# A fused attention and two-layer-pair kernel: one-bank PSUM tiles, attention batches in pairs, and shifted priorities

## The chip, the cores and the metric

The kernel runs on one core of a Trainium2 chip. The metric is the device time of one execution in microseconds. The profile is taken from one execution of its own, whose time stands beside its span below.

The engines are called as in the profile: PE is TensorE (PEld its weight loads), DVE is VectorE, ACT is ScalarE, POOL is GpSimd, and SP is SyncE, which issues nearly all DMAs here.

## The reference

Attention over 4 batches, 8 heads, 768 positions, 64 numbers per head, in chunks of 32 queries. Each chunk sees 8 memory slots and its own window of 16 + 32 + 8 keys:

```
scores = (q_c @ k_full.T) / 8            # 32 queries x 64 keys
a      = exp(scores - max(scores))
a      = a / (sum(a) + 1e-9)
out_c  = a @ v_full
x      = out, as 3072 tokens x 512
h = x @ w_in;   g = s * relu(h)**2 + b;           x = g @ w_out     # 512 -> 2048 -> 512
h = x @ w_in2;  g = h * sigmoid(1.702 * h);       y = g @ w_out2    # 512 -> 2048 -> 512
```

The weights come as float64. All results are float32 and are wanted to nearly that precision, so large products are made as three products of rounded parts (high x high, high x low, low x high).

## The kernel before

**Order.** Nothing runs in the order in which the code lists it. The class `Plan` collects operations: each has a due value (`need`), the engines that could do it with an assumed duration, what it comes after, and the buffers it takes. `Plan.order` (L80) then plays the program through with these durations, and writes the instructions out in the order it finds. Among the operations that could start on an engine within `PATIENCE` of the earliest, it takes the one with the smallest latest time (`late`). Operations with two engines go to the one that would end them first (for instance copies out of PSUM, L248). An attention batch is marked `dense`, and no two dense batches may start within `SPACE` = 2.4 us of the plan's clock. Where the plan sees TensorE idle before the first real accumulation, it puts in filler matmuls on a zero tile (`idle`, L1304).

**Attention.** A tile is 128 queries of all 8 heads; there are 24. `attend` (L427) handles one of the first four tiles alone and the later ones two at a time. A tile goes through these steps: loads of k, q and v (L439); scores `sc` on TensorE (L454); masking of the edge; the maximum `top` and its subtraction on VectorE (L471, L474); the exponential in place in `qe` on ScalarE (L479); transposes `pp` (L487); a copy to `px` (L249); the sum `den` (L497, L500, L501); the values `o` (L515); the division (L520); transposes `xx` back (L529); then high and low part, `xh` (L249) and `xl` (L546). The scores or values of one tile are 32 matmuls in the order listings and 64 in the trace, each using a 64x32 part of the array. q and k each have one buffer for a pair of tiles, so the next pair's q can be loaded once the transposes and the sum have read the exponentials.

**First layers.** Tokens are taken in blocks of 512 (`b`), four tiles each. `step` (L628) does one 128-wide piece j of the hidden layer for a block: 12 matmuls into `ph` (L644), ScalarE and VectorE make the gate (L650, L657, L654 or L661), split it into `gh` (L665) and `gl` (L669), and 12 matmuls add into `accA`, `accB` (L677). The first two j are done in halves of 256 tokens, so that they can start with tiles 0 and 1. Blocks are visited in the order 0, 1 (j below 8), 1, 0 (j from 8), 2, 3. Each weight piece is brought to a rounded high part and a low part by ScalarE and VectorE (`words` and `prep`, L334 to L400: four steps on VectorE, of which L346 is the last), just before it is needed.

**Later layers.** The last third of the first pair of layers and all of the second go through a Winograd-like scheme over 2 x 2 blocks with seven products (`wino`, L961, four runs `s` = 0 to 3). Products go from one accumulator to the next by a ScalarE copy (`seed`, L1059). `outer_product` (L1152) makes the last products; `away` (L1187) adds two parts (L1194) and stores them (L1201).

**PSUM.** Of eight banks two are `h`, two are `accA` as one tile, two are `accB` as two one-bank tiles, two are `a` as one tile. Attention takes `a`, tiles 1 and 3 take `accA` (`SIDE`).

Of the kernel before, what the change touches and what calls it, by code (L numbers as in the profile page):

```python
# [32 lines left out]
WARM = 8  # L33
# [12 lines left out]
S_PE = 0.8  # L46
V_PE = 0.8

class Plan:
# [3 lines left out]
    AFTER = {"pe": 0.2, "act": 0.05, "dve": 0.05, "pool": 0.2, "sp": 0.1, "aq": 0.1, "none": 0.0}  # L53
    OVER = {"act": 0.09, "dve": 0.08}
    BEAT = 0.24
    SPACE = 2.4
# [23 lines left out]
    def order(self):  # L80
# [20 lines left out]
        for i in range(len(ops) - 1, -1, -1):  # L101
# [7 lines left out]
            late[i] = self.due.get(i, min(due))  # L109

# [7 lines left out]
        holds, packed = {}, [-9.0]  # L118
# [25 lines left out]
        while left:  # L144
# [29 lines left out]
            if i in self.dense:  # L174
                packed[0] = t
# [20 lines left out]
        for i, e in chosen:  # L196
            if e == "pe":
                idle = min(starts[i], first) - clock
                if idle > 0.3:
                    full.append((None, int((idle - 0.3) / self.BEAT)))  # L200
                clock = ends[i]
            full.append((i, e))
# [13 lines left out]
def attention_moe_moe(ctx: ExitStack, tc: tile.TileContext, q_t, k_w, v_w, w_in1, w_out1, s_b, w_in2, w_out2, out):  # L216
# [13 lines left out]
    ps_a = ctx.enter_context(tc.tile_pool(name="ps_a", bufs=1, space=PS))  # L230
# [62 lines left out]
    o_cold = op(-999, {"dve": 0.7}, chill, alloc=[("ys", "cold")])  # L293
    plan.due[o_cold] = -1000.0
    o_ident = op(-135, {"pool": 0.5}, lambda e: make_identity(nc, ident))
# [8 lines left out]
    op(-999, {"pe": 0.46 * WARM}, warm, after=[o_cold], alloc=[("h", "warm")], uses=["cold"])  # L304


    managers = {"gp": pool_g, "att": pool_a}
# [115 lines left out]
    def bank(name, u):  # L423
        T[name, u] = (ps_acc if u in SIDE else ps_a).tile([P, 2, 512], F32, tag="accA" if u in SIDE else "a", name=name)
        return T[name, u]

    def attend(u):  # L427
# [3 lines left out]
        one = len(plan.ops)  # L431

# [48 lines left out]
        def turn(i):  # L481
            def fn(e):
                if i == 0:
                    bank("pp", u)
                x = T["qe", g][:, u[i] % 2]
                for a in range(HP):
# [8 lines left out]
        def total(e):  # L495
            den = T["den", u] = att.tile([P, n * HP, 2], F32, tag="den", name="den", bufs=2)
            nc.vector.tensor_reduce(  # L497
                out=den.rearrange("p x h -> p (x h)"), in_=T["qe", g][:, sub].rearrange("p t a (h s) -> p (t a h) s", h=2),
                op=ALU.add, axis=AX.X)
# [863 lines left out]
```

## Time and profile before

| | |
|---|---|
| time, median of 3 runs | 1084.7 us (1083.78 to 1085.21) |
| the profiled execution | 1084.78 us |
| its span in the trace | 1083.0 us |
| PE busy | 1063.8 us (98%) |
| PEld busy | 908.4 us (84%) |
| DVE busy | 763.4 us (70%) |
| ACT busy | 598.5 us (55%) |
| DMA | 265.68 MB, mean 245 GB/s |

The span runs from the first instruction of the program to its last; what the device time has beyond it lies around it. Busy time of TensorE includes matmuls that overlap, since they are pipelined, so it hides short gaps: starts of neighbouring matmuls tell more.

### The profile page before, as it was taken

To read this page: it belongs to the slowest core of one execution; us is meant where nothing else is said; L and a number is where in the kernel's file an instruction comes from. 1 tells how busy PE (TensorE), PEld (TensorE's weight loads), DVE (VectorE), ACT (ScalarE), POOL (GpSimd) and SP (SyncE) were. 2 spreads that over 40 slices of the span, in tenths; PEclk is the share of its full clock that TensorE was granted. 3 is DMA by queue.
4 is the path that set the end of the run, shared out by engine and by line. 5 is a ranking of instruction groups with operands and counts; after the bars stand their busy time and mean duration, and the time that the engine had idled before them with its cause. 6 is when DMAs were issued, how large, how long until landed. Compare 5 with 4: busy or idle time off the path is not lost.

```text
span 1083.0 us, 21691 instructions
## 1 busy us (share of the span) xinstructions
PE 1063.8 (98%) x8588; PEld 908.4 (84%) x8588; DVE 763.4 (70%) x1155; ACT 598.5 (55%) x921; POOL 0.7 (0%) x6
## 2 busy tenths in 40 slices
PE   8899999999999999999999999999999999999998
PEld 6777887778877788788888777999888999888998
DVE  7898986778798658888999554995223985222944
ACT  5668755545666647688744665543355532454432
POOL 0000000000000000000000000000000000000000
PEclk9999999999999999999999999999999999999999
DMA  9988934658699964888978998867656766666662
GB/s 341 313 279 295 304 125 142 229 180 304 212 328 313 371 222 152 308 298 271 326 225 282 340 346 283 262 203 252 195 185 212 235 196 221 193 187 205 196 204 79
DMA packets 151541, 265.68 MB, mean 245 GB/s; under 512 B 14224, under 2 KB 65424, under 8 KB 151440
## 3 DMA queue, kind: packets, MB, share of 16 engines
q1 hardware_dynamic: 151152, 263.77, 72.9%
q8 instruction: 68, 1.11, 0.4%
q10 hardware_dynamic: 288, 0.52, 0.1%
q14 instruction: 33, 0.27, 0.1%
HBM read 190.84 MB, written 73.40 MB: 244 GB/s over the span
## 4 chain that ended last, share of the span: by engine, by line
PE 88%; DMA 2%; ACT 2%; DVE 0%; SPq 0%; issue 0%; DVEq 0%
PE ph L644 14%; PE pc L1166 10%; PE accA L677 7%; PE accB L677 7%; PE pd L1166 6%; PE pb L1166 6%; PE pc L1172 3%; PE pd L1015 3%; PE pd L1017 3%; PE pd L1016 3%; PE ph L1015 3%; PE ph L1017 3%; PE ph L1016 3%; PE pc L1015 2%; PE pc L1017 2%; PE pc L1016 2%
## 5 line engine op out<-in xcount | busy, mean ns | idle before, releaser
L1140 DVE TENSOR_TENSOR oj<-G,oj 128x1024 fp32r<-128x1024 f32 x72 | 87.9, 1222 | 51.3 <-ACT oj L1137 50.8
L1137 ACT CAST oj<-G 128x1024 fp32r<-128x1024 f32 x72 | 75.6, 1051 | 87.5 <-PE pd L1166 28.6
L650 ACT ACTIVATE r<-ph 128x512 f32<-128x512 f32 (+1 forms) x66 | 38.5, 583 | 75.3 <-PE ph L644 68.8
L1137 ACT CAST oq<-G 128x1024 fp32r<-128x1024 f32 x40 | 42.1, 1052 | 51.6 <-PE pc L1166 22.0
L1140 DVE TENSOR_TENSOR oq<-G,oq 128x1024 fp32r<-128x1024 f32 x40 | 48.9, 1222 | 27.3 <-ACT oq L1137 27.3
L1166 PE MATMUL pc<-wih,oj 128*128 128x256 f32 x336 | 62.4, 284 | 0.0
L665 ACT CAST gh<-r 128x512 fp32r<-128x512 f32 (+1 forms) x66 | 40.0, 606 | 37.4 <-PE accB L677 34.9
L1149 DVE TENSOR_TENSOR G<-G 128x1024 f32<-128x1024 f32 x48 | 57.2, 1220 | 0.4
L669 DVE TENSOR_TENSOR gl<-r,gh 128x512 fp32r<-128x512 f32 (+1 forms) x66 | 44.1, 668 | 17.3 <-ACT gh L665 16.7
L368 ACT ACTIVATE u<-st 128x512 f32<-128x512 f32 x64 | 42.6, 670 | 22.8 <-DMA st<-w_in 12.9
L1027 ACT ACTIVATE G<-ys 128x512 f32<-128x512 f32 x64 | 40.6, 634 | 24.9 <-DVE ys L1069 24.4
L1166 PE MATMUL pd<-wih,oj 128*128 128x256 f32 x288 | 53.8, 284 | 0.0
L1166 PEld LDWEIGHTS pc<-wih,oj 128*128 128x128 f32 x336 | 53.3, 192 | 0.0
L1166 PE MATMUL pc<-wil,oj 128*128 128x256 f32 x168 | 47.6, 284 | 0.0
L1166 PEld LDWEIGHTS pd<-wih,oj 128*128 128x128 f32 x288 | 45.9, 192 | 0.0
L1166 PE MATMUL pc<-wih,oq 128*128 128x256 f32 x240 | 45.7, 284 | 0.0
L380 DVE SCALAR_TENSOR_TENSOR u<-u,st 128x512 uint32<-128x512 uint32 x64 | 43.4, 685 | 2.4 <-ACT st L376 1.4
L1166 PE MATMUL pb<-wih,oj 128*128 128x256 f32 x240 | 44.7, 284 | 0.0
L386 DVE SCALAR_TENSOR_TENSOR u<-st,u 128x512 uint32<-128x512 uint32 x64 | 43.5, 686 | 0.5
L376 ACT ACTIVATE st<-st 128x512 uint32<-128x512 uint32 x64 | 42.9, 672 | 0.8 <-DMA st<-w_out 0.7
L657 ACT ACTIVATE r<-r 128x512 f32<-128x512 f32 (+1 forms) x66 | 40.8, 618 | 1.6
L677 PE MATMUL accA<-gh,woh 128*128 128x512 f32 (+1 forms) x132 | 41.5, 390 | 0.0
(253 smaller groups left out, 3011.0 us busy)
## 6 DMA issues: line engine op xcount, KB each, us to landing
wih<-wodh SPq DMA_DIRECT2D x112, 256.0 KB, 2.9
wil<-wodl SPq DMA_DIRECT2D x112, 256.0 KB, 3.4
wih<-wch SPq DMA_DIRECT2D x96, 256.0 KB, 3.5
wil<-wcl SPq DMA_DIRECT2D x96, 256.0 KB, 3.9
st<-w_in SPq DMA_DIRECT2D x32, 512.0 KB, 6.5
st<-w_out SPq DMA_DIRECT2D x32, 512.0 KB, 6.0
k<-k_w SPq DMA_DIRECT2D x24, 512.0 KB, 5.4
v<-v_w SPq DMA_DIRECT2D x24, 512.0 KB, 5.9
```

Source lines behind the costliest of these rows:

```text
L380: nc.vector.scalar_tensor_tensor(out=u, in0=u, scalar=3, in1=T["st", i][:, :, 0], op0=ALU.logical_shift_left, op1=ALU.bitwise_or)
L386: nc.vector.scalar_tensor_tensor(out=u, in0=T["st", i][:, :, 1], scalar=0x80000000, in1=u, op0=ALU.bitwise_and, op1=ALU.bitwise_or)
L644: nc.tensor.matmul(T["ph", i], T[win][x][:, k * P:(k + 1) * P], T["x", m, b][y][:, k, r], start=seen_["hid"] == 1, stop=seen_["hid"] == 3 ...
L669: nc.vector.tensor_tensor(out=gl, in0=T["r", i], in1=gh.bitcast(F32), op=ALU.subtract)
L677: nc.tensor.matmul(T["acc", group, k // 2][:, k % 2][:, r], T[wout][x][:, k * P:k * P + P], T["g", i][y], start=fresh and (x, y) == (0, 0) ...
L1015: nc.tensor.matmul(ph, wh, xh, start=first and i == 0, stop=False, skip_group_check=True)
L1016: nc.tensor.matmul(ph, wh, xl, start=False, stop=False, skip_group_check=True)
L1017: nc.tensor.matmul(ph, wl, xh, start=False, stop=i == 1, skip_group_check=True)
L1137: nc.scalar.copy(out=T[kh], in_=g_of(ty, z))
L1140: nc.vector.tensor_tensor(out=T[kl], in0=g_of(ty, z), in1=T[kh].bitcast(F32), op=ALU.subtract)
L1149: o_raw[out, x] = [op(need, {"dve": 1.22}, lambda e: nc.vector.tensor_tensor(out=g_of(out, z), in0=g_of(a, z), in1=g_of(b, z), op=o), afte ...
L1166: nc.tensor.matmul(a, lt[:, z], rh, start=first and t % 2 == 0 and x == 0, stop=p == HALF - 1 and x == 2, skip_group_check=True)
```

## The change

- `WARM` goes from 8 to 9; the cold tile is set by one memset, without the cast; a new operation `table` runs an exponential of one column on ScalarE as soon as that tile is there.
- `HEADED = 1`: for tile 0 the subtraction, the exponential and the sum are replaced. VectorE scales the maximum by -1/8 (`bias`), and ScalarE does eight exponentials of 64 columns straight from PSUM with that bias, each adding up its sum (`heads`). The transposes of that tile may go two at a time. The later steps are as before.
- The spacing `SPACE` of dense batches is gone. Instead the plan charges 0.09 for going into one and 0.25 for coming out of one, with batches of 0.66 instead of 0.8.
- `bank` and `pair`: attention has its own pools `ps_a` and `ps_x`; when attention is over they are closed, and their banks become one-bank tiles `accA0`, `accA1`, `a0`, `a1` as `accB` already was.
- The last `outer_product` of the program is cut into two halves, and the last stores into one half and two quarters (`last`).
- Assumed durations change, and the table `SHIFTS` adds a number to the latest time of stretches of operations, so that the plan chooses another order.

```diff
-WARM = 8
+WARM = 9
+HEADED = 1
-S_PE = 0.8
-V_PE = 0.8
+S_PE = 0.66
+V_PE = 0.66
+SHIFTS = (
+    (894, 1, 7.29), (671, 4, -0.76), (408, 16, -0.4), (1809, 256, 4.91), (804, 4, -3.27), (1733, 1, 26.29),
...
-    SPACE = 2.4
+    INTO, OUT_OF = 0.09, 0.25
...
+        for at, n, by in SHIFTS:
+            for i in range(at, min(at + n, len(ops))):
+                shift[i] += by
+        late = [x + y for x, y in zip(late, shift)]
...
-            if i in self.dense:
-                t = max(t, packed[0] + self.SPACE)
+            if e == "pe" and (i in self.dense) != packed[0]:
+                t += self.OUT_OF if packed[0] else self.INTO
...
     def chill(e):
-        cold = pp.tile([P, KT, 512], F32, tag="ys", name="cold")
-        T["cold"] = cold[:, 1].bitcast(F32R)
-        fill(e, cold[:, 0], 0.0)
-        nc.vector.tensor_copy(out=T["cold"], in_=cold[:, 0])
+        T["cold"] = pp.tile([P, KT, 512], F32, tag="ys", name="cold")[:, 0].bitcast(F32R)
+        fill(e, T["cold"].bitcast(F32), 0.0)
+
+    def table(e):
+        x = const.tile([P, 1], F32, name="one")
+        nc.scalar.activation(out=x, in_=T["cold"].bitcast(F32)[:, :1], func=AF.Exp)
...
     def bank(name, u):
-        T[name, u] = (ps_acc if u in SIDE else ps_a).tile([P, 2, 512], F32, tag="accA" if u in SIDE else "a", name=name)
+        T[name, u] = (ps_x if u in SIDE else ps_a).tile([P, 2, 512], F32, tag="s", name=name)
...
+        def bias(e):
+            nc.vector.tensor_scalar_mul(out=T["top", u], in0=T["top", u], scalar1=-SCALE)
+
+        def heads(a):
+            def fn(e):
+                if a == 0:
+                    T["den", u] = att.tile([P, n * HP, 2], F32, tag="den", name="den", bufs=2)
+                x, sc = T["qe", g][:, u[0] % 2], two("sc")
+                for h in range(2):
+                    nc.scalar.activation(out=x[:, a, h * SLOTS:h * SLOTS + SLOTS], in_=sc[:, h, a], func=AF.Exp, scale=SCALE,
+                                         bias=T["top", u][:, h, a], accum_out=T["den", u][:, a, h:h + 1])
+            return fn
...
     def pair(tag, name):
-        if tag == "accB":
-            return Banks([ps_acc.tile([P, 512], F32, tag=f"{tag}{n}", name=name) for n in range(2)])
-        return (ps_a if tag == "a" else ps_acc).tile([P, 2, 512], F32, tag=tag, name=name)
+        pool = {"accB": ps_acc, "accA": pools.get("ps_y"), "a": pools.get("ps_b")}[tag]
+        return Banks([pool.tile([P, 512], F32, tag=f"{tag}{n}", name=name) for n in range(2)])
...
+        def last(n, b, part, need, after, end):
+            held = ("turn", s) + BANKS[n]
+            lo, hi = (part, part + 1) if b else (0, 2)
+            z = slice(256 * lo, 256 * hi)
+
+            def fn(e):
+                nc.vector.tensor_tensor(out=spot(b)[:, z], in0=T[held][:, b][:, z], in1=spot(b)[:, z], op=ALU.add)
+
+            def store(e):
+                r = bp * 512 + b * 256
+                dst = out[r + lo * P:r + hi * P, 256:512].rearrange("(t p) d -> p t d", p=P)
+                nc.sync.dma_start(out=dst, in_=spot(b)[:, z].rearrange("p (t d) -> p t d", t=hi - lo))
...
-                    prev = [outer_product(n, p, here + 8 * p, key, d, prev + wait)]
+                    if s == len(SEVEN) - 1 and n == 2 and p == HALF - 1:
+                        prev = [outer_product(n, p, here + 8 * p + only, key, d, prev + wait, only) for only in range(2)]
+                    else:
+                        prev = [outer_product(n, p, here + 8 * p, key, d, prev + wait)]
```

What the change moves, at three places. The first is the start, on TensorE, before (`warm` and `idle` are matmuls on the zero tile; `sc`, `pp`, `o`, `xx` are the steps of attention; a row of 32 is one tile):

```order
L1304 MATMUL idle<-cold 128x512 x5
L301 MATMUL warm<-cold 128x512 x8
L454 MATMUL sc<-k,qe 32x64 x32
L1304 MATMUL idle<-cold 128x512 x7
L454 MATMUL sc<-k,qe 32x64 x32
L487 MATMUL pp<-ident,qe 128x128 x4
L1304 MATMUL idle<-cold 128x512 x3
L515 MATMUL o<-v,px 32x64 x32
L1304 MATMUL idle<-cold 128x512 x3
L487 MATMUL pp<-ident,qe 128x128 x4
L529 MATMUL xx<-ident,px 128x128 x4
```

The same engine and place in the changed kernel (a row of 64 is two tiles):

```order
L361 MATMUL warm<-cold 128x512 x9
L515 MATMUL sc<-k,qe 32x64 x32
L1427 MATMUL idle<-cold 128x512
L515 MATMUL sc<-k,qe 32x64 x32
L1427 MATMUL idle<-cold 128x512 x6
L561 MATMUL pp<-ident,qe 128x128 x8
L1427 MATMUL idle<-cold 128x512
L592 MATMUL o<-v,px 32x64 x64
L606 MATMUL xx<-ident,px 128x128 x8
```

Transposes, values and back-transposes of tiles 0 and 1 now each stand together; before, tile 0 was through its values ahead of tile 1's transposes.

The second place is tiles 8 and 9, on TensorE, during the first visit of block 1 with j from 8 on (`ph` and `wj` belong to the hidden layer), before:

```order
L454 MATMUL sc<-k,qe 32x64 x32
L644 MATMUL ph<-xh_348,wj 128x512 x4
L644 MATMUL ph<-xl_349,wj 128x512 x4
L454 MATMUL sc<-k,qe 32x64 x32
L644 MATMUL ph<-xh_348,wj 128x512 x4
```

And now:

```order
L515 MATMUL sc<-k,qe 32x64 x64
L735 MATMUL ph<-xh_387,wj 128x512 x8
L735 MATMUL ph<-xl_388,wj 128x512 x4
L735 MATMUL ph<-xh_387,wj 128x512 x4
L561 MATMUL pp<-ident,qe 128x128 x8
L735 MATMUL ph<-xl_388,wj 128x512 x4
L735 MATMUL ph<-xh_387,wj 128x512 x4
L592 MATMUL o<-v,px 32x64 x64
```

Eight large matmuls stood between the two scores; now the scores of both tiles stand together, and so do the values.

The third place is the end, on VectorE, before (`oj`, `oq` are split operands, `ys` holds the outputs, `pc` the last accumulator):

```order
L1140 TENSOR_TENSOR oj_11644<-G_5698,oj_11643 128x1024
L1182 TENSOR_TENSOR ys_10328<-pd_11533,ys_10328 128x512
L1182 TENSOR_TENSOR ys_10328<-pd_11534,ys_10328 128x512
L1194 TENSOR_TENSOR ys_10328<-ys_10328 128x512 x2
L1140 TENSOR_TENSOR oj_11673<-G_5698,oj_11672 128x1024
L1140 TENSOR_TENSOR oq_11707<-G_5698,oq_11706 128x1024
L1194 TENSOR_TENSOR ys_10328<-pc_11659,ys_10328 128x512 x2
```

And now:

```order
L1231 TENSOR_TENSOR oq_11741<-G_5690,oq_11740 128x1024
L1273 TENSOR_TENSOR ys_10375<-pd_11588,ys_10375 128x512
L1231 TENSOR_TENSOR oj_11757<-G_5690,oj_11756 128x1024
L1273 TENSOR_TENSOR ys_10375<-pd_11589,ys_10375 128x512
L1285 TENSOR_TENSOR ys_10375<-ys_10375 128x512 x2
L1310 TENSOR_TENSOR ys_10375<-pc_11703,ys_10375 128x256 x2
L1310 TENSOR_TENSOR ys_10375<-pc_11702,ys_10375 128x512
```

The two last additions read one two-bank tile; now two quarters of one bank are added first and the other bank last, and on TensorE the last six matmuls write that other bank alone.

## Rows read from the trace of the kernel before

**Rows 1.** Table of stretches: start:end, length, busy us of each engine, clock, DMA.

```profile
0.00:8.00 8.00, 6.09 (x78) 4.69 (x78) 0.91 (x2) 2.45 (x3) 0.70 (x6) 1.00 0.78 288
8.00:20.00 12.00, 10.33 (x231) 7.32 (x232) 11.64 (x25) 6.42 (x12) 0.00 (x0) 1.00 1.03 386
20.00:38.00 18.00, 14.13 (x316) 11.01 (x315) 14.95 (x31) 12.01 (x24) 0.00 (x0) 0.91 0.91 315
...
60.00:92.00 32.00, 31.56 (x446) 24.41 (x445) 28.33 (x49) 21.63 (x37) 0.00 (x0) 1.00 0.91 297
...
680.00:1078.00 398.00, 398.00 (x2698) 369.77 (x2697) 223.84 (x247) 173.60 (x237) 0.00 (x0) 1.00 0.64 202
```

**Rows 2.** List of TensorE's waits: who waited for whom, sum, times, longest.

```profile
PE o L515 <- issue: 1.9, 1, 1.9
...
PE pd L1015 <- ACT pd L1059: 1.3, 2, 0.7
```

**Rows 3.** Instructions in order of time, the start: start, length, engine, line, operands.

```profile
7.11 0.86 PE L454 MATMUL sc<-k,qe 64*32 64x64 f32 x64
...
13.64 0.63 ACT L479 ACTIVATE qe<-qe 128x512 f32<-128x512 f32 x1
...
19.65 0.74 PE L644 MATMUL ph<-xh,wih 128*128 128x256 f32 x4 [0.20 <-ACT xh L249]
```

**Rows 4.** The same view, tiles 2 and 3.

```profile
24.04 0.86 PE L454 MATMUL sc<-k,qe 64*32 64x64 f32 x64
...
26.75 0.34 PE L515 MATMUL o<-v,px 64*32 64x64 f32 x12 [0.44 <-ACT px L249]
...
28.94 0.75 PE L515 MATMUL o<-v,px 64*32 64x64 f32 x52 [1.85 <-issue]
...
36.80 0.74 PE L644 MATMUL ph<-xh,wih 128*128 128x256 f32 x4 [0.20 <-ACT xh L249]
```

**Rows 5.** The same view, TensorE around one lone attention batch.

```profile
203.81 0.62 PE L677 MATMUL accA<-gh,wol 128*128 128x512 f32 x2
204.26 0.61 PE L677 MATMUL accB<-gh,wol 128*128 128x512 f32 x2
204.81 0.86 PE L454 MATMUL sc<-k,qe 64*32 64x64 f32 x64
205.59 0.74 PE L677 MATMUL accA<-gh,woh 128*128 128x512 f32 x2
206.18 0.63 PE L677 MATMUL accB<-gh,woh 128*128 128x512 f32 x2
```

**Rows 6.** ScalarE's groups by shape: count, busy us, mean ns, idle before.

```profile
L479 ACT ACTIVATE qe<-qe 128x1024 f32<-128x1024 f32 x10 | 10.5, 1055 | 4.4 <-DVE qe L474 4.4
...
L479 ACT ACTIVATE qe<-qe 128x512 f32<-128x512 f32 x4 | 2.5, 628 | 2.7 <-issue 1.7 <-DVE qe L474 1.0
...
L650 ACT ACTIVATE r<-ph 128x256 f32<-128x256 f32 x4 | 1.5, 377 | 1.1 <-ACT st L376 0.7 <-PE ph L644 0.4
```

**Rows 7.** Instructions in order of time, at the entry to block 1.

```profile
88.42 1.29 DVE L546 TENSOR_TENSOR xl<-xx,xh 128x512 fp32r<-128x512 f32 x2 [0.81 <-ACT xh L249]
...
88.44 1.20 PE L644 MATMUL ph<-xh,wih 128*128 128x512 f32 x4 [0.24 <-ACT xh L249]
```

**Rows 8.** VectorE's groups by shape, 0 to 90 us.

```profile
L346 DVE TENSOR_TENSOR wol<-u,woh 128x512 fp32r<-128x512 f32 x8 | 5.5, 686 | 0.7 <-ACT woh L249 0.7
...
L661 DVE TENSOR_SCALAR r<-r,sb 128x512 f32<-128x512 f32 x5 | 2.7, 541 | 0.9 <-ACT r L657 0.9
L474 DVE TENSOR_TENSOR qe<-sc,top 128x512 f32<-128x512 f32 x4 | 2.7, 676 | 0.0
```

**Rows 9.** Instructions in order of time, the end.

```profile
1078.38 1.29 DVE L1194 TENSOR_TENSOR ys<-pc,ys 128x512 f32<-128x512 f32 x2 [6.45 <-PE pc L1166]
1079.10 0.97 SPq L1201 DMA_DIRECT2D out<-ys  x2
```

**Rows 10.** The page's DMA queues: packets, MB, share of 16 engines.

```profile
q8 instruction: 68, 1.11, 0.4%
```

More of the change, by code (lines that the diff above doesn't have):

```diff
@@ L198, in order @@
                 idle = min(starts[i], first) - clock
-                if idle > 0.3:
-                    full.append((None, int((idle - 0.3) / self.BEAT)))
+                if clock and idle > 0.3:
+                    full.append((None, int((idle - 0.3) / (self.SLOW if clock < self.COLD else self.BEAT))))
                 clock = ends[i]
@@ L596, in attend @@
         for i in ids if b > 3 else ():
-            z = op(px + 1, {"act": 0.6, "dve": 0.5}, whole(i), after=[bk[i]], uses=[("xx", u), ("px", g)])
+            z = op(px + 1, {"act": 0.59, "dve": 0.69}, whole(i), after=list(bk), uses=[("xx", u), ("px", g)])
             o_xd.append(op(px + 1, {"sp": 0.8}, away(i), after=[z], uses=[("px", g)]))
@@ L1161, in fn @@
                 if m:
-                    for t in range(4):
+                    for t in range(4) if only is None else range(2 * only, 2 * only + 2):
                         z = slice(t * P, t * P + P)
@@ L1173, in fn @@
                                              stop=p == HALF - 1 and x == 2, skip_group_check=True)
-            return op(need, {"pe": 1.45 if m else 1.36}, fn, after=o_part[n, p // 2] + [d] + after, alloc=taken(tag, held),
+            return op(need, {"pe": 0.72 if only is not None else 1.44 if m else 1.36}, fn, after=o_part[n, p // 2] + [d] + after, alloc=taken(tag, held),
                       uses=[("wp", s, n, p // 2), key + ("h",), key + ("l",), held])
@@ L1211, in away @@
             return d
+        def last(n, b, part, need, after, end):
[8 more added lines that the diff above has]
+                nc.sync.dma_start(out=dst, in_=spot(b)[:, z].rearrange("p (t d) -> p t d", t=hi - lo))
+            d = op(need, {"dve": 0.42 if b else 0.69}, fn, after=[end] + after, uses=[tmp, held])
+            o = op(need, {"sp": 0.37 if b else 0.73}, store, after=[d], uses=[tmp])
+            plan.soon.update((d, o))
         kept = [x for z in (s_12, s_22) for y in z.values() for x in y]
@@ L1254, in wino @@
                 elif n == 2:
-                    away(n, b, b, e, [got["u4", b], got["c22", b]], False, False, b)
+                    if s == len(SEVEN) - 1:
+                        for part in range(b + 1):
+                            last(n, b, part, e, [got["u4", b], got["c22", b]], o_end[n][b])
+                    else:
+                        away(n, b, b, e, [got["u4", b], got["c22", b]], False, False, b)
         for x in range(HALF // 2):
@@ L1258, in wino @@
             free_g[3, x], free_g[1, x] = o_part[5, x] + o_raw[2, x], o_part[2, x]
+    side_ops = []
     for u in parts:
         if u[0] < 8:
+            one = len(plan.ops)
             attend(u)
+            if u in SIDE:
+                side_ops.extend(range(one, len(plan.ops)))
+    o_y_pool = [op(-1, {"none": 0.0}, follow("ps_x", "ps_y", bufs=1, space=PS), after=side_ops)]
     for i in range(2 * NF):
@@ L1279, in attention_moe_moe, with swap @@
             attend(u)
-    o_late = [op(-1, {"none": 0.0}, follow("att", "late", bufs=1, side="right"), after=stage_ops)]
+    def swap(e):
+        follow("att", "late", bufs=1, side="right")(e)
+        follow("ps_a", "ps_b", bufs=1, space=PS, side="right")(e)
+    o_late = [op(-1, {"none": 0.0}, swap, after=stage_ops)]
     wo_ops = []
```

83 lines of the change are left out of this document (54 added, 29 removed), and 43 rows, old and new, of the table SHIFTS.

## The prediction

> **What bounds the kernel now.** I read the table of stretches first. TensorE is busy in all of 680 to 1078 us, so the change can give nothing there. From 0 to 38 us it is idle for 7.5 us (8.00 + 12.00 + 18.00 less 6.09 + 10.33 + 14.13). Between 60 and 92 us TensorE (31.56 of 32.00) and VectorE (28.33 of 32.00) are both close to full: there two engines bound the time together [rows 1]. Then the list of waits: in the whole run no entry of TensorE sums to more than 1.9 us [rows 2]. So a gain must come from four places: the first stage, the price of TensorE's own changes of shape, the handovers through ScalarE, and the end.
>
> Then the instructions in order of time. At the start the scores of tile 0 begin at 7.11 us, tile 1's exponential at 13.64, the first large product (ph) at 19.65 [rows 3]. Tile 3's scores stand at 24.04; its neighbour's values stop after 12 of 64 small matmuls at 27.09 and go on at 28.94; the first product of tiles 2 and 3 comes at 36.80 [rows 4].
>
> Later on, a lone attention batch (64 small matmuls) stands between matmuls of 512 columns [rows 5]. Undisturbed, two of these take 0.45 us (203.81 to 204.26). The two ahead of the batch take 0.55, the batch 0.78, the two behind it 0.59: a lone batch costs 0.10 + 0.78 + 0.14 = 1.02 us. Twelve small matmuls show 0.34 [rows 4] and 64 show 0.86, so one is 10 ns and 64 are 0.64. The other 0.38 is entering and leaving.
>
> **The pairs.** The order has 48 separate attention stretches before and 25 now; 23 batches lose their 0.38. Of these, 16 belong to tiles 8 to 23, which run where TensorE is the bound: 16 x 0.38 = 6.1; I count 0.37, since a seam between two batches may not be quite free: **5.9 us**. Should the slow pair of matmuls behind a batch (0.14) stay, it is 16 x 0.24 = 3.8. The other seven lie in the first 92 us and count below.
>
> **The start.** Now the second k load stands ahead of the first weight, the loads for tiles 2 and 3 ahead of the weight stores, and two tiles go together.
>
> The head-by-head softmax puts eight ACTIVATEs of 64 columns in place of a subtraction (0.68) and an exponential (0.63). No row has that shape. The exponentials of 512 and 1024 columns give 0.20 fixed and 0.83 ns per column [rows 6], so 0.25 each and 2.0 for eight. Ends: 0.08 each, in proportion to 512 columns (0.6), and 0.38, the 256-column row (3.0). I take 2.0, nearest to the only rows of this function. The chain of tile 0 becomes 0.7 us longer (-0.7 to +1.7). Tile 1's exponential waits only for these: with scores at 7.11, their 0.86, and about 1.2 for mask, maximum and its scaling, the eight end near 11.2, and it starts there instead of at 13.64. ScalarE then has a weight step and both copies in front of it; I put the first ph at 19.2. Three groups of four matmuls (at most 0.74 each [rows 3]) stand between it and the scores of tiles 2 and 3, which end near 22, against 24.9 for tile 3 before.
>
> On this the Trainium skill has a rule that speaks against the change ("Advanced Engine Details and Errata", The Read-Write Bubble): a gap is exposed with every instruction, so tiles of 512 or 1024 elements are better. The fixed 0.20 of rows 6 agrees. By that rule alone the eight would be a loss of 0.7 us; by the rows they are beside the path that decides.
>
> That path is VectorE. The second visit waits for tile 7's xl, at 88.42, and TensorE itself waits 0.24 there for xh [rows 7]. Up to that xl VectorE has 135 instructions in the order before, 129 now. Missing are tile 0's subtraction and sum, one weight remainder, one gl, one copy (five passes over 128x512 at 0.68) and one affine (0.54); a scaling of 8 numbers is new, at about 0.2: 3.7 us [rows 8]. The cast of the cold tile is gone too, but lay in the wait for the first scores and is worth nothing. VectorE idled 10.5 us in the first 38 us (7.1 + 0.4 + 3.0) [rows 1]; laying out the new chain by hand I get 0.7 more, since it waits while ScalarE does the heads. 3.7 - 0.7 = **3.0 us**. Ends: 0, if TensorE's clock falls to 1.2 GHz in the waits ahead of the first values (in 20 to 38 us the granted share was 0.91 on average [rows 1]) and each step of the chain is late; and 6.4, if TensorE's path decided: 3.0 from the scores, 1.9 from the stop, 4 x 0.38 from tiles 4 to 7. I take VectorE's figure because rows 1 and 7 show it as the one waited for.
>
> **The end.** Before, two additions (1.29 us) follow the last matmul, and the second store is issued behind both [rows 9]. Now the bank of the last tile's second half is finished six matmuls earlier; behind the last matmul stands one addition of 0.65 with at most 0.2 of a quarter addition ahead. The last store goes 0.5 us earlier and has two half-size stores ahead of it instead of a full one: **0.7 us** (0.3 to 1.0).
>
> **Costed at nothing.** The early table load: the first scores, which come at 7.11 us, hide it before and now; uncovered, it would show as later first scores. One-bank tiles let half a tile go earlier; the largest late waits are handovers through one ScalarE copy (pd: two, 1.3 us [rows 2]), where the next product needs that copy anyway. In the order the tight ones (a product directly behind the copy's source) are three before and four now: 0, from -2 (three more at 0.7) to +1.5 (the first ones go, since one ScalarE step fewer stands ahead). One more store on SP is in the 0.7. The real matmuls stay the same (3169 of 512 columns, 2112 of 256), and the filler ones, 35 before and 19 now, lie in idle time.
>
> **Sum.** 5.9 + 3.0 + 0.7 = 9.6. The profiled execution took 1084.78 us (span 1083.0 and 1.8 around it), 0.1 from the median of 1084.7. Forecast: **1075.2 us**.
>
> **Rivals.**
> A. *The start pays in full*: TensorE's path decides, not VectorE's. For it: 7.5 us of idle TensorE up to 38. Against: VectorE is 89% busy from 60 to 92. 5.9 + 6.4 + 0.7 = 13.0: 1071.8.
> B. *VectorE eats the start*: weights are only as early as VectorE, and it gains nothing. For it: by tile 3's xl only two weights are ready now, four before. 5.9 + 0.7 = 6.6: 1078.2.
> C. *Starved pairs, slower*: the stop at 27.09 ended with no engine named ("issue" [rows 2, 4]). Instructions themselves are fetched by DMA, 68 times, 16 KB each (1.11 MB / 68) [rows 10], and two batches had just been issued. A pair issues twice as many in one go. Price 1.85 each, six such stops eat the gain (9.6 / 1.85 = 5.2), and if every second of the 23 pairs stops, 12 x 1.85 = 22: 1097. Against: from tile 8 on at least 32 larger matmuls stand between scores and values of a pair, and of 48 batches before only one stopped.
> The Trainium skill ("Runtime: NRT & Kernel Launch", Instruction fetch mechanics) holds the crossing of a 16 KiB block for mostly hidden, as issue is slower than the fill. By it C is out and this stop something else; the row at 28.94 speaks against it, once in 48 batches.
> D. *New handovers*: the new order makes TensorE wait for ScalarE copies behind 680 us, where it never waited. Nine of 0.7 us: 6.3 lost, 1081.5; twelve and none of the start: no change. For it: the order of products is shuffled there too. Against: nearly every product keeps another one between itself and its source.
>
> **Chances and range.** Forecast 0.48 (its own range 1073 to 1077.5), A 0.20, B 0.20, C 0.06, D 0.06. The measurement tells about 0.2% (2.2 us) from no change: forecast, A and B are faster, D is mostly no change, C slower: 0.88, 0.06, 0.06. The range holds A and B, a us below A for early handovers that go, and almost reaches D: 1070.5 to 1081.
>
> **What would show it.** Pairs: 25 attention stretches, a pair about 1.66 us instead of 2.04. Start: first ph near 19, first product of tiles 2 and 3 near 31, tile 7's xl about 3 us before 88.42; between 60 and 90 TensorE then waits for weights or xl if VectorE is the bound. End: 0.7 us less between the last matmul and the end. C would be long "issue" waits at o or sc, D waits of ph, pb, pc or pd for ScalarE copies behind 680 us. I am wrong if the stage up to 92 us is not shorter, or if a pair costs as much as two lone batches.

## The result, and the profile after

The changed kernel takes 1065.21 us (median of 4, 1064.97 to 1065.36), the kernel before 1084.42 beside it: ratio 0.9822, interval [0.9805, 0.9839]. The gain is 19.2 us; 9.5 was forecast, and 1065.2 lies 5.3 us below the range. The direction was right and the size was not.

The profiled execution took 1065.36 us (span 1063.4). To see where 19.6 us of span went, I took in both traces the time at which TensorE had done the same amount of real work (matmuls of 512, 256 and 128 columns and the small ones at 227, 120, 109 and 10 ns, fillers left out):

| stage (work done) | before | after | gained there | forecast |
|---|---|---|---|---|
| start, to the second block (60 us) | 90.33 | 84.79 | 5.5 | 3.0 |
| tiles 8 to 23 (to 400 us) | 446.02 | 432.19 | 8.3 | 5.9 |
| the products that follow (to 650 us) | 702.43 | 683.39 | 5.2 | 0 |
| to the last matmul | 1078.06 | 1059.16 | -0.1 | 0 |
| behind the last matmul | 4.93 | 4.19 | 0.7 | 0.7 |

The table of stretches after, with the columns of [rows 1]:

```profile
0.00:8.00 8.00, 6.55 (x139) 4.75 (x140) 1.63 (x5) 1.62 (x3) 0.70 (x6) 1.00 0.79 298
8.00:20.00 12.00, 10.01 (x268) 7.79 (x268) 9.63 (x20) 9.80 (x31) 0.00 (x0) 1.00 1.03 401
20.00:38.00 18.00, 16.94 (x410) 14.86 (x391) 15.57 (x34) 11.34 (x24) 0.00 (x0) 1.00 0.93 312
60.00:92.00 32.00, 30.17 (x382) 24.71 (x368) 30.69 (x54) 27.76 (x49) 0.00 (x0) 1.00 0.96 328
680.00:1058.00 378.00, 377.78 (x2541) 350.04 (x2540) 205.10 (x224) 164.71 (x226) 0.00 (x0) 1.00 0.63 199
```

TensorE's idle time up to 38 us is down from 7.5 to 4.5 us, most of it between 20 and 38, where the granted clock is now 1.00 instead of 0.91. From 60 to 92 us TensorE waits 1.8 us instead of 0.4. The list of TensorE's waits, as in [rows 2]:

```profile
PE ph L735 <- ACT wih L306: 3.3, 3, 1.5
PE o L592 <- ACT px L306: 1.7, 3, 1.3
...
PE o L592 <- issue: 0.7, 2, 0.4
```

(In the changed kernel L306 is the helper that copies and casts, L735 and L768 are the first layers' products, L1106 to L1108 the later ones, L1150 and L1154 ScalarE's copies out of their accumulators; L1015, L1059 and L1063 before. `ph`, `pb`, `pc` and `pd` are accumulators in PSUM.) The stop of 1.9 at o is gone, and so are all the waits of products for ScalarE's copies behind 446 us. New are three waits for weights (wih), at 38.7 and 61.1 us above all. In order of time, beside [rows 3, 4]:

```profile
5.59 0.99 PE L515 MATMUL sc<-k,qe 64*32 64x64 f32 x64
...
17.41 0.74 PE L735 MATMUL ph<-xh,wih 128*128 128x256 f32 x4 [0.34 <-ACT wih L306]
19.04 1.51 PE L515 MATMUL sc<-k,qe 64*32 64x64 f32 x128
24.51 1.51 PE L592 MATMUL o<-v,px 64*32 64x64 f32 x128
28.44 0.74 PE L735 MATMUL ph<-xh,wih 128*128 128x256 f32 x4
```

The first scores are 1.5 us earlier (I had left them at 7.11), the first ph 2.2, the first product of tiles 2 and 3 8.4. At equal work 4.6 of these 8.4 us are lost again at the waits at 38.7, 44.0 (1.3 at o) and 61.1 us, and 1.7 won back up to the second block, which leaves 5.5. A pair later on, beside [rows 5]:

```profile
253.52 0.61 PE L768 MATMUL accB<-gh,wol 128*128 128x512 f32 x2
254.07 1.51 PE L515 MATMUL sc<-k,qe 64*32 64x64 f32 x128
255.50 1.20 PE L735 MATMUL ph<-xh,wih 128*128 128x512 f32 x4
```

Computed as for the lone batch, the median pair of 16 adds 1.641 us, the median lone batch of 32 before 1.006: 2 x 1.006 - 1.641 = 0.371 for each pair. The 0.37 was exact; that 0.38 less a guess of 0.01 meets it so closely is luck.

### The profile page after: what moved, and what is told of

It reads as the page before. It is cut to its first block, busy times and chain, and to the rows that moved or that the text cites. A ratio compares the mean times of both kernels' runs of the same rounds, so it can differ in the third digit from the quotient of the medians.

```text
span 1063.4 us, 21658 instructions
## 1 busy us (share of the span) xinstructions
PE 1049.5 (99%) x8573; PEld 904.7 (85%) x8573; DVE 761.0 (72%) x1148; ACT 603.0 (57%) x943; POOL 0.7 (0%) x6
## 4 chain that ended last, share of the span: by engine, by line
PE 94%; DMA 2%; DVE 2%; ACT 1%; issue 1%; SPq 0%; ACTq 0%; DVEq 0%
PE ph L735 16%; PE pc L1257 10%; PE accA L768 8%; PE accB L768 8%; PE pd L1257 7%; PE pb L1257 6%; PE pc L1263 3%; PE ph L1106 3%; PE pd L1106 3%; PE ph L1108 3%; PE ph L1107 3%; PE pd L1107 3%; PE pd L1108 3%; PE pd L1263 2%; PE pb L1263 2%; PE pc L1106 2%
## 5 line engine op out<-in xcount | busy, mean ns | idle before, releaser
L768 PE MATMUL accA<-gh,woh 128*128 128x512 f32 (+1 forms) x132 | 41.9, 392 | 0.2 <-ACT gh L756 0.2
## 6 DMA issues: line engine op xcount, KB each, us to landing
wih<-wodh SPq DMA_DIRECT2D x112, 256.0 KB, 2.9
wil<-wodl SPq DMA_DIRECT2D x112, 256.0 KB, 3.4
wih<-wch SPq DMA_DIRECT2D x96, 256.0 KB, 3.7
wil<-wcl SPq DMA_DIRECT2D x96, 256.0 KB, 4.0
```

The costliest lines, as they stand in the source:

```text
L768: nc.tensor.matmul(T["acc", group, k // 2][:, k % 2][:, r], T[wout][x][:, k * P:k * P + P], T["g", i][y], start=fresh and (x, y) == (0, 0) ...
```

## The experiments

Each ratio is to the kernel before, measured beside it. The expectations number their theories: 1 is the tile, 2 the pairs, 3 VectorE as the bound of the first stage, 4 the table load, 5 the earlier first scores, 6 the transfers. The entry is the time of 60 us of real work, that is, of the second block: 84.8 in the changed kernel, 90.3 before. Some kernels vary much from run to run (the changed kernel by 0.4 us, the one without shifts by 8.2), and one execution of each is traced, so what one edit does at one place is read from the traces, at equal work.

**The tile: two banks back, and one bank alone.**

```
 changed kernel, pair():
-    return Banks([pool.tile([P, 512], F32, tag=f"{tag}{n}", name=name) for n in range(2)])
+    ... if tag == "accB" else pool.tile([P, 2, 512], F32, tag=tag, name=name)
```

> The changed kernel with one thing undone: accA and a (the second product of a pair beside the fourth, and the accumulators of the second layers) are again one tile over two PSUM banks. Every engine issues the same instructions in the same order as the changed kernel. Theory 1 (the tile): between 400 and 650 us the changed kernel lost its waits of pd, pc and ph for the ScalarE copies because a copy no longer has to wait for the product in the other bank of its tile; then about 5.2 us come back (1070.4 us), as waits of the products for L1150. Rival (the order): these waits went because the shifted priorities put other work between a product and its copy; then 1065.2 within 0.7 us, and no wait of a product for L1150 above 0.3 us.

Measured: 1071.76 us, ratio 0.9872 [0.9851, 0.9893]. Between 400 and 650 us of work it loses 5.6 us, and 0.7 behind the last matmul. The list of TensorE's waits from 400 to 700 us, which is empty in the changed kernel:

```profile
PE ph L1106 <- ACT ph L1150: 2.5, 3, 1.2
PE pd L1106 <- ACT pd L1150: 0.7, 1, 0.7
PE pc L1106 <- ACT pc L1150: 0.7, 1, 0.7
```

The list sums to 3.9 us and counts a stop too low: the largest is 1.16 in it and 1.4 at equal work. That one in order of time, in this run:

```profile
653.58 0.39 PE L1107 MATMUL pb<-xl,wih 128*128 128x512 f32 x1
...
653.81 0.39 PE L1108 MATMUL pb<-xl,wil 128*128 128x512 f32 x1
654.23 0.59 ACT L1154 COPY ys<-pb 128x512 f32<-128x512 f32 x1 [1.77 <-PE pb L1108]
654.71 0.59 ACT L1150 COPY ph<-pb 128x512 f32<-128x512 f32 x1
...
655.36 0.50 PE L1106 MATMUL ph<-xh,wih 128*128 128x512 f32 x1 [1.16 <-ACT ph L1150]
```

and the same place in the changed kernel:

```profile
648.41 0.59 ACT L1154 COPY ys<-pb 128x512 f32<-128x512 f32 x1 [0.41 <-PE pb L1108]
648.43 0.39 PE L1107 MATMUL pb<-xl,wih 128*128 128x512 f32 x1
...
648.89 0.59 ACT L1150 COPY ph<-pb 128x512 f32<-128x512 f32 x1
...
649.34 0.39 PE L1108 MATMUL pb<-xl,wil 128*128 128x512 f32 x1
...
649.57 0.47 PE L1106 MATMUL ph<-xh,wih 128*128 128x512 f32 x1
```

The same instructions in the same order. With one-bank tiles both copies run beside the six matmuls into the other bank of pb; with a two-bank tile they wait until the last of those is done. The wait in the tile's name belonged to the neighbour bank.

The opposite, the kernel before with one-bank tiles:

> The kernel before with one thing added: accA and a as two tiles of one bank, attention's two-bank tiles in a pool of their own that is closed first. Every engine issues the same instructions in the same order as the kernel before. Theory 1 (the tile): the waits at 449, 609, 636, 657 and 667 us go: about 4.8 us less, 1079.6 us. Rival (the order): 1084.4 within 0.7 us, with those waits in place.

Measured: 1081.41 us, ratio 0.9966 [0.9952, 0.9979]. Between 400 and 650 us of work it gains 2.6 us, and 0.6 at the end. The rest of this trace's difference is stops elsewhere: 1.2 us lost ahead of the second block (0.9 at o, at 62.6 us), 1.9 gained in tiles 8 to 23. Left are waits that its order really makes:

```profile
PE ph L1015 <- ACT pb L1059: 0.7, 1, 0.7
PE pd L1015 <- ACT pd L1059: 0.7, 1, 0.7
PE pb L1015 <- ACT ys L1063: 0.6, 1, 0.6
```

So theory 1 holds for half of the 5.2 us in the old order; the other half needs both. For these 250 us of work the old order takes 256.4 us with two banks and 253.8 with one, the new order 256.8 and 251.2: the order alone gives nothing.

**The pairs undone, and alone.**

```
-S_PE = 0.66
-V_PE = 0.66
+S_PE = 0.8
+V_PE = 0.8
...
-    INTO, OUT_OF = 0.09, 0.25
+    SPACE = 2.4
```

> The changed kernel with the rule of before for attention batches (at least 2.4 us from one start to the next, 0.8 us for a batch) in place of the price for entering and leaving: lone batches again, shifts and the rest as in the changed kernel. Theory 2: 48 attention stretches again, each of 23 more costs 0.37: 16 of them in tiles 8 to 23 are 5.9 us, the seven of the start are hidden behind VectorE: 1071.1 us. Rival: the seven count as well, 8.5 us: 1073.7. A second rival: what the pairs bring from 160 to 446 us is not the entering and leaving but the stops that vanish there (3.1 us before, 0.6 after); then about 1067.7.

Measured: 1073.49 us, ratio 0.9887 [0.9864, 0.9909]. From 60 to 400 us of work it loses 7.6 us: 16 x 0.37 = 5.9, and stops of 0.5 (326 us) and 1.4 (341 us) that the lone order brings. At the entry it is 2.8 us late, but this is not the price of seven pairs, since the planner lays out the start anew. At 34 us it is 4.7 late (the granted clock is at half from 19.0 to 22.4 us); by 65 us it is 0.5 ahead, as it has none of the waits for wih at 38.7 and 61.1; and the 2.8 arise between 67 and 88 us, with waits of 0.7 (accA), 0.8 (pp) and 0.6 (wih) beside the lone batches.

> The kernel before with one rule replaced: the price for entering and leaving attention in place of the 2.4 us between batches (and 0.66 us for a batch); no shifts, two-bank tiles, old softmax and end. Theory 2 (entering and leaving, priced at 0.37 for each of 23 batches): 16 x 0.37 = 5.9 us in tiles 8 to 23, and in the first stage up to 7 x 0.37 = 2.6 more, as the run with lone batches in the changed kernel showed 2.8 there; 1076 to 1078.5 us. Rival (pairs need the shifts): without them pairs are starved or make long waits like the four of 1.2 to 2.5 us that stood at 357 to 368 us in the run without shifts; 1083 us or more.

Measured: 1080.23 us, ratio 0.9953 [0.9937, 0.9969]. From 60 to 400 us it gains 8.45 us, all that the changed kernel gains there, without shifts. Of the 2.5 above 5.9, 1.8 are stops at lone batches: TensorE's waits from 187 to 446 us sum to 2.3 before and 0.5 here. The largest of them (1.1 at 362 us) is chance: two other traces of the same order, those without early fillers and with deferred stores, don't have it. Up to 54 us this run is 5 us ahead of the kernel before, but the entry comes 3.9 us later, above all behind this:

```profile
61.65 1.29 PE L454 MATMUL sc<-k,qe 64*32 64x64 f32 x103
66.65 0.65 PE L454 MATMUL sc<-k,qe 64*32 64x64 f32 x25 [3.70 <-issue]
```

A pair of scores stops after 103 of 128 matmuls for 3.7 us. A 16 KB transfer of the instruction queue began at 64.4 us and took 0.95; TensorE goes on 1.3 us after its end. The granted clock is then at half from 65.8 to 72.7 us. This is rival C, priced at 1.85 for each stop, and only in the first stage: behind 92 us no pair of this run stops for more than 0.7.

> The kernel before with the pairs (the price for entering and leaving) and the one-bank tiles together; the order is that of the run with the pairs alone. Theories 1 and 2, if they add: the run with pairs alone was 4.0 us shorter, its waits of pd, pc and ph for the ScalarE copies (0.97, 1.76, 0.82, 0.82, 0.82 at 445 to 664 us) go as far as they are the other bank's, 3 to 5 us, and 0.6 at the end: 1074.5 to 1077 us by the trace. Rival: as in the kernel before with one-bank tiles, only 2.8 of them go, and the first stage loses more: 1077 to 1079.

Measured: 1078.38 us, ratio 0.9941 [0.9922, 0.9961], in the rival's range; its profiled execution 1075.2, in that of theories 1 and 2. In this trace they add: 8.3 from 60 to 400, 2.2 from 400 to 650, 0.8 at the end, less 1.8 at the entry, where the same pair of scores stops again, for 1.8 us (to 65.7 us, 1.2 after the end of a transfer of instructions).

**The shifts.** The table empty, `SHIFTS = ()`:

> The changed kernel with the table of shifted priorities empty; the planner's rules, the pairs, the one-bank tiles and the head-by-head softmax stay. Theory 1: the shifts are worth the stops of 0.4 to 1.3 us that before had between 187 and 361 us and part of the first stage: 2 to 4 us, 1067 to 1069, and the handovers from 400 to 650 us stay away. Rival (the order): the handovers come back, at least 5 us: 1070 or more.

Measured: 1081.76 us, ratio 0.9974 [0.9957, 0.9991]. The traced execution (1078.81) is the fastest of ten; where the median's other 3 us lie, no trace shows. In it the entry is 0.3 us later, so there the shifts give the start next to nothing. 8.4 us are lost at the last pair (357 to 369 us), where the granted clock is at half from 361.6 to 368.4 us, and 4.8 between 400 and 650 us of work, 3.6 of them in two handovers (444 and 451 us). The list of waits from 350 to 455 us begins:

```profile
PE pp L561 <- ACT qe L540: 2.3, 1, 2.3
PE pb L1106 <- ACT ys L1154: 1.7, 1, 1.7
PE o L592 <- DVE px L306: 1.4, 1, 1.4
PE ph L1106 <- ACT pb L1150: 1.4, 1, 1.4
```

Without shifts the new rules leave the last pair's exponential, copies and division with no product beside them, which neither theory had; the rival was right on two handovers. With shifts and lone batches the stretch from 400 to 650 us of work takes 251.0 us, with pairs and no shifts 256.0, so the order that goes without waits on one-bank tiles is the work of the shifts.

**The parts of the start.** Tile 0 with one subtraction, one exponential and one sum, first laid out anew by the planner, then in exactly the old places:

```
-    nc.vector.tensor_scalar_mul(out=T["top", u], ...)      (scaling)
+    less(e)                                                (subtraction)
-    for h in range(2): nc.scalar.activation(...)           (eight)
+    exp(e)                                                 (one, at the first place)
```

> The changed kernel with the softmax of tile 0 as in the kernel before (one subtraction, one exponential, one sum); the shifts keep their steps, all else is as in the changed kernel. Theory 3 (VectorE sets the first stage): VectorE gets back a subtraction and a sum (0.68 each) less a scaling of 8 numbers (0.17): 1.2 us at the entry of the second block; 1066.4 us, with tile 7's xl about 1.2 us later. Rival A (the path of tile 0 sets it): the eight ACTIVATEs took 2.3 us in place of 1.3, so without them tile 0 is earlier and the time is the same or up to 1 us less. Rival B: the chain of tiles 0 and 1 counts in full; over 3 us more.

Measured: 1073.94 us, ratio 0.9890 [0.9869, 0.9911]; the entry 6.8 us later with other waits (2.8 us for wih at 82 us, 2.3 inside scores at 32 us, a stop like that of rival C). The planner moved everything, so this says nothing on the heads.

> The changed kernel with tile 0's softmax computed by one subtraction (in the place of the scaling), one exponential (in the place of the first of the eight ACTIVATEs) and one sum, every other instruction on every engine in the same order. Theory 3 (VectorE's work sets the entry of the second block): VectorE has 0.52 + 0.68 = 1.2 us more to do, the entry comes 1.2 us later, 1066.4 us. Rival (the first values set it): the eight ACTIVATEs took 2.3 us, the subtraction and one exponential take 0.52 + 0.63 = 1.15 more than the scaling alone, so tile 0 is 1.1 us earlier, and tile 1's exponential too: same time or up to 0.5 less. (The run that had the planner order this anew lost 6.8 us in the first stage, but it moved everything else as well.)

Measured: 1064.58 us, ratio 0.9807 [0.9792, 0.9823], the entry 0.3 us later. The head-by-head softmax is worth nothing that can be told. Its price, in the changed kernel:

```profile
L551 ACT ACTIVATE qe<-sc,top 128x64 f32<-128x64 f32 x8 | 2.4, 325 | 4.7 <-PE sc L515 4.7
...
L551 ACT ACTIVATION_READ_ACCUMULATOR qe<-sc,top 128x1 f32 x8 | 1.7, 217 | 0.0
```

Eight take 2.3 us from 7.86 to 10.19, as each sum is a second instruction; 2.0 was estimated.

The old start (cast, 8 warming matmuls, no table load), no table load alone, and before without its five early fillers:

> The changed kernel with the start of before: the cold tile is cast (one more pass on VectorE ahead of the warming matmuls), 8 of them instead of 9, one filler matmul more, no early table load; every engine's order is otherwise that of the changed kernel. First scores near 7.0 us instead of 5.59. Theory 3 (VectorE, busy in all but 1 us from 38 us on, sets the end of the stage): the delay of 1.4 us stands in VectorE's idle time at the start and comes out in full at the second block: 1066.6. Rival (slack): the waits for weights at 38.7, 44.0 and 61.1 us (4.8 us in all) swallow it: within 0.4 us of 1065.2.

> The changed kernel without the early table load; every other instruction in the same order. The table load then comes ahead of tile 0's first exponential. Theory 4: since the scores now start at 5.59 us, the load (1.3 us) is no longer hidden and the exponentials of tile 0 start up to 0.5 to 1.3 us later than 7.86; whether it comes out at the end of the stage is the same question as for the old start: up to 1066.5 if VectorE sets it, 1065.2 if there is slack.

> The kernel before without the five filler matmuls that stand ahead of its eight warming ones; every other instruction in the same order. First scores near 5.6 us instead of 7.11. Theory 5: of the 5.55 us that the changed kernel is ahead at the second block, the earlier scores bring up to 1.5 if TensorE's path sets the stage (1083.0), and 0.5 or less if weights and VectorE do (1084.4 within 0.5), as the run with the old start gave back 0.5 of its 1.2 us before the second block.

Measured: 1065.85, ratio 0.9818 [0.9799, 0.9838], entry 0.7 us later; 1065.98, 0.9819 [0.9799, 0.9839], entry 0.2 earlier, though the load stands ahead of the first exponential; 1084.55, 0.9994 [0.9984, 1.0004], scores 1.5 earlier and the entry 0.1. The old start did not delay the first scores as expected (5.62 us, against 5.59), but tile 0's exponentials, by 1.2 us, of which 0.7 arrive at the second block; without the early load they are 1.0 later, and nothing arrives.

**What sets the entry: VectorE or the transfers.** Nine of VectorE's subtractions on GpSimd:

```
-    nc.vector.tensor_tensor(out=lo, ...)
+    (nc.gpsimd if o and j < 9 else nc.vector).tensor_tensor(out=lo, ...)
```

> The changed kernel with the first nine remainders wol (0.69 us each on VectorE, all in the first 92 us) computed by GpSimd, which is idle; every other instruction in the same order. Theory 3 (VectorE sets the first stage): 6.2 us of its work go; the entry of the second block comes 2 to 5 us earlier (the waits for wih on ScalarE then bound it), 1060 to 1063. Rival A (ScalarE and the loads set it, VectorE only looks full): within 0.7 us of 1065.2. Rival B (GpSimd's subtraction, whose price no row shows, comes too late for its product or slows VectorE): slower, 1066 or more, with waits of accA for wol.

Measured: 1066.87, ratio 0.9836 [0.9816, 0.9856], the entry 2.6 us later: rival B, it seems by way of a slower VectorE (the wait for wih at 61.1 us grows from 1.5 to 2.4), since the products wait for wol 0.2 us only.

```profile
L406 POOL TENSOR_TENSOR wol<-u,woh 128x512 fp32r<-128x512 f32 x9 | 15.0, 1662 | 78.7 <-ACT woh L306 66.2 <-DVE woh L306 12.6
```

One takes 1.66 us instead of 0.69, and VectorE's own passes beside it are slower (gl of 512 columns 861 ns, 682 without).

> The changed kernel with the stores of the first layer's weights (6.1 MB of the 28.8 that are moved before the second block begins) issued only once its first product stands in TensorE's queue, one behind each later transfer; all else in the same order. Theory 6 (the transfers set the first stage: share 0.93 to 0.99, 28.8 MB at 340 GB/s are 84.7 us): 22.7 MB would take 67 us, so another bound comes first; TensorE has 75.8 us of work up to there and its waits for first values (about 5 us up to 30 us) stay: entry at 80 to 81.5 instead of 84.8, 3 to 4.5 us less: 1060.7 to 1062.2, if the stores that come later cost nothing there. Rival A (VectorE and ScalarE set it): the entry within 0.5 us of 84.8, 1065.2. Rival B: the entry is earlier, but the stores delay the loads of the second block's weights and attention; 1065 or more.

> The changed kernel with four of the weight stores of the first stage issued twice, the second time to a place that nothing reads: 1.05 MB more (4 x 262 KB) before the second block begins; all else in the same order. Theory 6: 1.05 MB at 340 GB/s: the entry 3.1 us later, 1068.3 us. Rival A: there is room between transfers (the waits of the queue for buffers are 30 us in all from 20 to 92 us), entry within 0.5 us, 1065.2.

> The kernel before with the same edit: stores of the first layer's weights behind the entry of the second block. Theory 6: before's stage is 90.3 us at 314 GB/s, share 0.90 to 0.93, with SP's queue held by stores that wait (9.8 us for wih between 20 and 92 us); without them the entry comes 3 to 6 us earlier: 1078.5 to 1081.5 us; and the stop inside tile 3's values (1.85 us, put down to issue) shrinks, as instructions come by the same transfers. Rival A (the engines and the order set it): entry within 0.5 us, 1084.5.

Measured, in this order: 1070.72, ratio 0.9874 [0.9858, 0.9891]; 1065.26, 0.9827 [0.9812, 0.9842]; 1086.57, 1.0015 [1.0003, 1.0026]. Theory 6 falls for the changed kernel. With the stores gone the transfers were no longer full. First the changed kernel, then the run without them:

```profile
38.00:60.00 22.00, 19.09 (x235) 14.86 (x241) 21.49 (x37) 15.28 (x27) 0.00 (x0) 1.00 0.97 334
60.00:85.00 25.00, 23.17 (x351) 18.90 (x337) 23.76 (x41) 21.36 (x37) 0.00 (x0) 1.00 0.99 349
```

```profile
38.00:60.00 22.00, 18.62 (x213) 14.82 (x211) 21.67 (x38) 14.88 (x26) 0.00 (x0) 1.00 0.72 239
60.00:85.00 25.00, 23.14 (x352) 18.72 (x351) 23.91 (x41) 21.23 (x37) 0.00 (x0) 1.00 0.76 251
```

and the entry came 0.4 us later; with 1.05 MB more it came 0.1 earlier. The late stores then cost 6.5 us (accA waits 3.8 us at 124 us). In before the deferred stores moved the entry of the profiled execution, the fastest of ten, 2.3 us earlier, all of it from one place: the values that stopped for 1.85 us [rows 4] run through, and the granted clock stays at its higher level (2.4 GHz), where before it was at half from 30.2 to 33.6 us:

```profile
27.40 0.87 PE L515 MATMUL o<-v,px 64*32 64x64 f32 x64 [0.45 <-ACT px L249]
```

From 38 us of time to the entry this lead stays the same. The third transfer of instructions began at 25.1 us here and at 26.5 in the kernel before, whose values stopped at 27.1. The later stores take 1.0 us back in this trace; why the median is 2.0 us above the kernel before, no trace shows.

VectorE's work alone, less (no clamp for twelve weights: `m == 0 and 3 <= j < 9 or nc.vector.tensor_scalar(...)`) and more (`wol` of six weights computed twice):

> The changed kernel without the clamp (0.42 us on VectorE each) of twelve weights, 3 to 8 of both layers, whose preparation lies between about 35 and 85 us: the clamp of very small and very large weights is left out there. All else in the same order. Theory 3 (from 38 us on VectorE, 97% busy, sets the entry of the second block): 12 x 0.42 = 5.0 us less work: the entry 3 to 5 us earlier (81 instead of 84.8), 1060.5 to 1062. Rival (ScalarE's chain of weights and the places in the order set it): under 1 us.

> The changed kernel with the remainder wol of the weights 3 to 8 computed twice in a row on VectorE (six more passes of 0.69 us, the same values). All else in the same order. Theory 3: 6 x 0.69 = 4.1 us more work and 3.3 us of idle time that isn't all in the right place: the entry 3 to 4 us later, 1068.2 to 1069.3. Rival (ScalarE and the order): the entry under 1 us later.

Measured: 1066.00, ratio 0.9830 [0.9816, 0.9845], the entry 0.4 us later; 1067.05, 0.9845 [0.9828, 0.9861], the entry 2.3 later. Work taken away from VectorE counts for nothing: the waits for wih at 38.7 and 61.1 us sum to 3.0 as in the changed kernel. Of the 4.1 us added, 1.2 come out where the second of these waits grows to 2.6, and 1.2 more behind it, where the granted clock is at half from 64.6 to 68.0 us. So VectorE's work alone doesn't set the entry.

**The end.** One addition for each half and two stores again (`if s == len(SEVEN) - 1` made false):

> The changed kernel with the end of before: one addition for each half of the last output behind the whole last product, two stores instead of three. By the prediction 0.7 us longer (0.3 to 1.0): 1065.9, all of it behind the last matmul. Rival: the store that is issued last has the same wait for the other stores, nothing changes.

Measured: 1065.02, ratio 0.9814 [0.9798, 0.9830]; 4.17 us behind the last matmul, 4.19 with the split. The split gives nothing. Instructions in order of time, first the end of the changed kernel, then of the run with two-bank tiles and the split:

```profile
1058.77 1.41 DVE L1310 TENSOR_TENSOR ys<-pc,ys 128x256 f32<-128x256 f32 x3 [3.64 <-PE pc L1257]
...
1059.16 0.28 PE L1257 MATMUL pc<-wih,oq 128*128 128x256 f32 x1
1059.22 1.37 SPq L1315 DMA_DIRECT2D out<-ys  x3
```

```profile
1064.91 0.28 PE L1257 MATMUL pc<-wih,oq 128*128 128x256 f32 x1
1065.23 1.35 DVE L1310 TENSOR_TENSOR ys<-pc,ys 128x256 f32<-128x256 f32 x3 [4.36 <-PE pc L1257]
1065.68 1.32 SPq L1315 DMA_DIRECT2D out<-ys  x3
```

The additions start 0.4 us ahead of the last matmul with one bank and 0.3 behind its start with two. The tail is 4.92 to 4.94 us in every run with two-bank tiles and 4.17 to 4.35 with one-bank ones.

## Why the prediction was right and wrong

**Costed at nothing: the one-bank tiles (failed).** This is the largest error: 5.2 us between the entries of rows for 446 and 702 us, and the 0.7 of the end as well. The step was "the next product needs that copy anyway". It does, but the copy had waited for the product in the other bank of the tile, which nobody needs. The count of tight handovers, three before and four now, was set to 0 too; the shifted order is worth 2.6 of the 5.2, on one-bank tiles alone. I weighed one entry (pd, 1.3 us [rows 2]); the waits for L1059 from 400 to 710 us sum to 4.0:

```profile
PE pd L1015 <- ACT pd L1059: 1.3, 2, 0.7
PE pc L1015 <- ACT pc L1059: 1.2, 1, 1.2
PE ph L1015 <- ACT pb L1059: 0.8, 1, 0.8
PE ph L1015 <- ACT ph L1059: 0.7, 1, 0.7
```

My end of +1.5 for "the first ones go" was too near.

On this the Trainium skill has a rule that I did not weigh ("PSUM — Partial Sum Buffer", Summary: rules for kernel authors): while matmuls run, read from a different bank, and guard by bank. By it a guard for two banks is more than the chip asks for; the rows at 648.41 us (one bank) and 654.23 us (two) agree.

**The end (right in size, wrong in cause).** 0.7 forecast, 0.74 measured; it is the tile that lets the first half start early, not the split.

**The pairs (mechanism and price right, too narrow).** 0.371 measured for 0.37, 16 pairs, 5.9. That lone batches also bring stops (2.3 us before, 1.1 of them by chance, 0.4 to 0.5 with pairs) was left out, since I took each as its own and not as what a batch between two products brings.

**The start (failed in size and in its sign of idle time).** The step was "I take VectorE's figure": 3.7 less work, 0.7 more idle time up to tile 7's xl. The stretches up to that xl, before (88.42 us) and after (82.01):

```profile
0.00:88.42 88.42, 80.44 (x1359) 63.70 (x1359) 72.38 (x134) 56.64 (x100) 0.70 (x6) 0.98 0.91 313
```

```profile
0.00:82.01 82.01, 72.77 (x1338) 58.70 (x1339) 69.55 (x129) 56.55 (x113) 0.70 (x6) 1.00 0.96 338
```

VectorE has 2.8 us less work (3.7 forecast) and 3.6 us less idle time (16.0 to 12.5; 0.7 more forecast). The sign that I named for VectorE came, a wait for weights between 60 and 90 us (1.5 at 61.1), and yet less VectorE work moved nothing. One thing reached the entry that I had held to be hidden: the stop at 27.09 us with the half clock behind it (2.3 us, by the one trace with deferred stores). It stood in rival A, and I cut it off because VectorE was 89% busy; in the kernel before, TensorE is idle 0.7 us in all from 38 to 90 us, so little stands behind the stop that could take it up. In the changed kernel much does: of the 4.7 us that the lone batches are late at 34 us nothing is left by 65 us, as the waits at 38.7 and 61.1 us shrink. Rival A's 6.4 was nearer to 5.5 than the forecast's 3.0, but not by its sum: tiles 2 and 3 gain 8.4, and waits for weights and values take much of it back. What the pairs of the start are worth by themselves is not shown.

What else sets the entry now is open. Less work for VectorE, fewer or more transfers, later first exponentials and another softmax moved it by 0.7 us at most; only more work on VectorE, slower VectorE passes, lone batches and the planner's new layout made it late. ScalarE's order, whose weights are waited for at 38.7 and 61.1 us, was not tried alone.

**The rivals.** B was wrong. C's mechanism is real: the stop before, 3.7 us with the pairs alone, 1.8 with pairs and one-bank tiles; the changed kernel has no issue wait at o above 0.4. In all 20 traces TensorE stops 40 times for 0.4 us or more with no semaphore to wait for, and each time it goes on 1.1 to 1.6 us after the end of a 16 KB transfer of the instruction queue. The Trainium skill ("Runtime: NRT & Kernel Launch", Instruction fetch mechanics) calls the crossing of such a block mostly hidden; behind 92 us the traces agree (eleven of the 40 stops, of 1.2 us at most); in the first stage they don't. That busy transfers are the reason is not shown: the transfer takes 0.96 us in the median of the kernel before, ahead of 92 us and behind it. D's waits behind 680 us did not come.

No run beat the changed kernel by more than these measurements can tell; tile 0 without heads (1064.58) is its equal.

## What to carry over

Before a wait for a copy is called needed, look at what the copy waited for: here a tile of two banks made the reader of one wait for the writer of the other. Whether a delay reaches the end of a stage is asked of the waits that stand behind it, and not of how full another engine is: 2.3 us came through in the kernel before, 4.7 were taken up in the changed one. Where several waits have one cause, sum the whole list, not its largest entry.

## What was not expected of the hardware

A sum taken along with an exponential is a second instruction on ScalarE (217 ns by the records, 0.29 us from one pair to the next for 64 columns). GpSimd's 128x512 subtraction takes 1.66 us and slows VectorE's passes beside it from 682 to 861 ns. A transfer of instructions that came late went with a stop of TensorE of 1.85 us before and 3.7 in one run; TensorE went on 1.5 and 1.3 us after its end.
